# The place of the output weights' load on GpSimd's queue: ahead of the cast of x of pair 3, or behind the scaling of pair 4

## The chip, the cores and the metric

One core of one Trainium2 chip. The metric is the device time of one execution in microseconds (us); of the kernel before there are three such times, and their median is what the changed kernel is held against. Engines are named as the profile names them: PE is TensorE (matmuls), DVE is VectorE, ACT is ScalarE, POOL is GpSimd, SP is SyncE. "SPq" and "POOLq" are the instruction queues of SP and POOL where they issue transfers.

## The reference

Two layers, one behind the other. The first is a linear attention with decay over x (4 batches, 8 heads, 768 tokens, 32 values a head), with B and C of 16 states a head and a decay a for each token. It is computed in chunks: with `cum` the running sum of log a, and causal L = exp(cum_i - cum_j),

```
y_i   = sum_{j<=i} (C_i . B_j) L_ij x_j  +  exp(cum_i) C_i . state
state = decay_full * state + sum_j decay_from_j * B_j x_j
```

The second takes the 3072 tokens of y, 256 wide (heads times values), through a gated feed-forward layer of width 1536:

```
out = (relu(y @ w_gate) * (y @ w_val)) @ w_out
```

`w_out` (1536 x 256) is the matrix whose load the change moves. All inputs and the output are float32; the kernel computes in bfloat16 with float32 sums.

## The kernel before, in words

**Tiling.** Tokens go in 12 pairs of 128-token chunks (256 tokens; three pairs to a batch) through the attention, and in 6 blocks of 512 tokens (two pairs) through the feed-forward layer. For each pair: x and B, C are loaded, B and C are scaled by decays, turned so that the states lie on the partitions, `G` forms C.B (tile `g`, PE), `gevac` masks it (tile `gs`; on ACT with a causal select on POOL, line 611, and on DVE), `Dm` and `inter` form y, and `astep`/`state` adds to the carried state `A_ps`. For a block, `gv`/`gvp` make gate and val (lines 783, 786, 812), ACT takes the relu, DVE multiplies into `h`, and `fout` (line 843) forms `out` from `h` and the output weights, the tile `wo`.

**Three ways to turn B and C.** Pairs 0 to 3 are turned by PE (`turn`). Pairs 4 and 5 are turned by a transposing transfer: `scale_bc` (POOL, lines 458 and 462) writes the scaled B and C of the pair into a tile `pad`, and `dturn` (line 479, on SP's queue) turns `pad` into `TT`, which `G` of that pair reads. Pairs 6 to 11 go by `seq_scale`, `seq_turn` and `seq_part`, from the tiles `seqB` and `seqC`.

**Order.** Nothing is scheduled by a planner. The order of every engine is the order of the lines of the kernel's body, written out by hand, and `in_order` at the end pins each engine to it. So an instruction that waits holds up everything behind it on its engine; that holds for transfers as well, since a transfer is issued by an instruction of the engine named (`nc.sync.dma_start` is SP's, `nc.gpsimd.dma_start` is POOL's).

**Transfers.** SP issues nearly all loads and all stores, on one hardware queue (q1 in the profile). POOL issues the feed-forward weights, which are cast from float32 to bfloat16 on the way, on a software queue (q0): `weights` for wg and wv (line 209) in five pieces, and `weights_out(0, NF)` (line 213) for all of `wo`, 768 KB in bfloat16, in one transfer. Whoever reads any part of `wo` waits for the whole transfer.

**The stretch around the change**, lines 1020 to 1085, in the order of each engine:

- SP: `load_wide(3)`, `load_x(3)`, `load_bc(4)`, `load_bc(5)` (C and two halves of B of pairs 4 and 5, lines 117 and 121), then `load_x(4)` (line 95, two transfers), `dturn(4)`, `load_x(5)`, `load_seq(2)` (`seqB`, `seqC`, line 134), `dturn(5)`, and the loads of pair 6.
- POOL: `scale_bc(3)` (line 469), the load of `wo`, the cast of x of pair 3 (`cast_x`, line 504), the scaling of pair 4 into its `pad`, three causal selects of pair 3 (line 611), some 3 us of small set-up work for the later pairs (`seq_start`, `seq_masks`), the cast of x of pair 4, `seq_decay` (line 377), the scaling of pair 5 into its `pad`, the cast of x of pair 5.
- PE: gate and val of blocks 0 and 1 with the attention of pairs 2 and 3 between them; then the first `outs(0, 0)`, which is the first reader of `wo`; `state(4, 0)` and `G(4)`; more of `outs`; `section(4, 5)`, in which `G(5)` is; and so on to the end.

Of the kernel before, what the change touches and what calls it, by code (L numbers as in the profile page):

```python
# [29 lines left out]
def kernel(  # L30
# [21 lines left out]
    NF = DF // 128  # L52
# [35 lines left out]
    def load_x(p, hold=False, q1=nc.sync):  # L88
        b, c0 = p // PPB, 2 * (p % PPB)
        xr = raw.tile([128, 2, NH, D], FP32, tag="xr", name="xr")  # L90
        if hold:
            nc.vector.memset(xr[0:1, 0, 0, 0:1], 0.0)
        for i in range(2):
            cs = slice((c0 + i) * 128, (c0 + i + 1) * 128)
            (q1 if i else nc.sync).dma_start(  # L95
                out=xr[:, i], in_=x[b, :, cs, :].rearrange("h s d -> s h d"))
        st[p]["xr"] = xr
# [114 lines left out]
    def weights_out(f0, f1):  # L212
        nc.gpsimd.dma_start(
            out=wo[:, f0:f1, :],
            in_=moe_w_out[f0 * 128:f1 * 128, :].rearrange("(o i) m -> i o m", i=128))
# [78 lines left out]
    def diag(t, slot):  # L294

        v = t[:, slot, 0:16]
        return bass.AP(v.tensor, v.offset, [v.ap[0], (32, 4), (144, 2), (1, 16)])

    def turned(p):
        return NWIDE <= p < NRUN  # L300
# [140 lines left out]
    def scale_bc(p, eng):  # L441
        b, c0 = p // PPB, 2 * (p % PPB)
        s = st[p]
        if p >= NRUN:
            bs = att.tile([128, 2, 128], BF16, tag="bt", name="bt")
            for t in range(2):
                hs = slice(4 * t, 4 * t + 4)
                eng.tensor_tensor(
                    out=bs.rearrange("s i (q t n) -> s i t q n", q=4, t=2)[:, :, t],
                    in0=s["br"][:, :, hs],  # L450
                    in1=scaleBC[:, b, c0:c0 + 2, 0, hs].unsqueeze(3).to_broadcast(
                        [128, 2, 4, N]), op=ALU.mult)
            s["B"] = [bs[:, i] for i in range(2)]
            return
        if turned(p):
            s["pad"] = t = pads[p - NWIDE]
            for i in range(2):
                eng.tensor_tensor(
                    out=diag(t, 2 * i), in0=s["br"][:, i].rearrange("s (q t) n -> s q t n", t=2),
                    in1=scaleBC[:, b, c0 + i, 0].rearrange("s (q t) -> s q t", t=2).to_broadcast(  # L460
                        [128, 4, 2, N]), op=ALU.mult)
            eng.tensor_tensor(
                out=t[:, 4:6].rearrange("s r (h n) -> s r h n", n=N),
                in0=s["cr"].rearrange("s h r n -> s r h n"),
                in1=wD[:, p % PPB, :, 8 * b:8 * b + 8].to_broadcast([128, 2, NH, N]), op=ALU.mult)
            return
        bs = att.tile([128, 4, 128], BF16, tag="bs", name="bs")
        src = s["bcr"].rearrange("s h j r n -> s (j r) h n")
        eng.tensor_tensor(
            out=bs.rearrange("s k (h n) -> s k h n", h=NH), in0=src,  # L470
            in1=factors[p].to_broadcast([128, 4, NH, N]), op=ALU.mult)
        s["tin"] = [[bs[:, 2 * j + r] for r in range(2)] for j in range(2)]
        s["sort"] = s["tin"][0]

    def dturn(p):

        s = st[p]
        s["TT"] = att.tile([128, 6, 128], BF16, tag="TT", name="TT", bufs=2)
        nc.sync.dma_start_transpose(out=s["TT"], in_=s["pad"].rearrange("s k m -> s (k m)"))
# [21 lines left out]
    def cast_x(p, ceng):  # L501
        cast = ceng.copy if ceng is nc.scalar else ceng.tensor_copy
        xb = x_tile(p)
        cast(xb, st[p]["xr"].rearrange("s i h d -> s (i h d)"))  # L504
# [539 lines left out]
    gevac(2, 3)  # L1044
    gv_evac(*u)
    scale_bc(3, nc.gpsimd)
    weights_out(0, NF)
    cast_x(3, nc.gpsimd)
    scale_bc(4, nc.gpsimd)
    load_x(4)  # L1050
    dturn(4)
    load_x(5)
# [138 lines left out]
```

## Time and profile before

| what | value |
|---|---|
| time of the kernel before, median of 3 (lowest, highest) | 122.97 us (122.79, 123.65) |
| the profiled execution's own time | 124.32 us |
| its span, first to last instruction | 122.6 us |
| PE busy | 116.4 us, 95% of the span |
| DVE, ACT, POOL busy | 91.4, 73.9, 50.9 us |
| granted TensorE clock | full in all 40 slices of the span |
| load of `wo`, issue to landing | 768 KB, 9.7 us |

Busy time of an engine says how much it worked, and not whether anybody waited for it. The page's chain of work gives the share of the span for which each line was the last to be waited for; the timeline gives start and length of each instruction, and in brackets how long the engine had been idle before it and who ended that. Rows of the transfer queues count packets; their shares can add up to more than 100%, since packets of the two queues overlap on an engine.

### The profile page before, as it was taken

How to read it: one execution, taken by the hardware profiler on the slowest of the kernel's cores; microseconds unless marked ns; L12 is line 12 of the kernel's file. 1: busy time of each engine (PE TensorE's matmuls, PEld its weight loads, DVE VectorE, ACT ScalarE, POOL GpSimd, SP SyncE). 2: the span in 40 equal slices, each digit the busy share in tenths (PEclk: the TensorE clock that was granted, in tenths of full speed). 3: DMA queues.
4: the chain of work that ended last, by engine and by line, in shares of the span. 5: the costliest groups of instructions: out<-in, count | busy, mean ns of one | idle time of the engine just before them, and what ended most of it. 6: DMA issues, size and time to landing. Idle time of an engine off the chain costs nothing.

```text
span 122.6 us, 3330 instructions
## 1 busy us (share of the span) xinstructions
PE 116.4 (95%) x1257; PEld 78.8 (64%) x1257; DVE 91.4 (75%) x197; ACT 73.9 (60%) x147; POOL 50.9 (42%) x108
## 2 busy tenths in 40 slices
PE   7899999999999969999999999999999999999980
PEld 5576674588888758644488544588444687444870
DVE  5897999889998259699796898893897850787320
ACT  4478579888764243776745766646667735766320
POOL 7999635979355964514760820031600030000000
PEclk9999999999999999999999999999999999999999
DMA  2999997999988978979995290003100003100022
GB/s 55 200 204 203 207 201 120 139 116 186 112 150 209 216 125 133 176 148 294 158 131 118 80 125 9 5 0 134 43 3 0 0 5 128 43 0 0 2 88 86
DMA packets 63088, 13.34 MB, mean 109 GB/s; under 512 B 54688, under 2 KB 63072, under 8 KB 63072
## 3 DMA queue, kind: packets, MB, share of 16 engines
q1 hardware_dynamic: 55152, 10.33, 45.7%
q0 software_dynamic: 4272, 2.36, 14.1%
q10 hardware_dynamic: 3648, 0.44, 2.4%
q8 instruction: 10, 0.16, 0.6%
q14 instruction: 6, 0.05, 0.2%
HBM read 11.94 MB, written 3.15 MB: 123 GB/s over the span
## 4 chain that ended last, share of the span: by engine, by line
PE 68%; DMA 15%; POOL 8%; SPq 4%; ACT 1%; issue 1%; POOLq 0%; ACTq 0%
PE o L843 21%; PE gate L783 18%; PE val L786 18%; DMA TT<-pad 5%; DMA wg<-in_moe_w_gate_dram 5%; DMA xr<-in_x_dram 5%; SPq L95 3%; PE g L600 2%; PE y L745 2%; PE gate L812 2%; PE val L812 1%; POOL wg L209 1%; POOL wv L209 1%; SPq L121 1%; PE o L878 1%; PE y L735 1%
## 5 line engine op out<-in xcount | busy, mean ns | idle before, releaser
L798 DVE TENSOR_TENSOR h<-r,val 128x512 bf16<-128x512 bf16 x54 | 36.2, 684 | 11.8 <-ACT r L794 11.3
L794 ACT ACTIVATE r<-gate 128x512 bf16<-128x512 f32 x54 | 32.1, 599 | 11.8 <-PE gate L783 11.6
L783 PE MATMUL gate<-yT,wg 128*128 128x512 bf16 x108 | 32.1, 379 | 0.0
L843 PE MATMUL o<-wo,h 128*128 128x256 bf16 x276 | 32.1, 273 | 0.0
L786 PE MATMUL val<-yT,wv 128*128 128x512 bf16 x108 | 32.1, 379 | 0.0
L843 PEld LDWEIGHTS <-h 128*128 128x128 bf16 x276 | 26.3, 98 | 4.0
L611 POOL TENSOR_SCALAR_AFFINE_SELECT gs<-gs 128x512 bf16<-128x512 bf16 (+1 forms) x25 | 12.9, 542 | 32.4 <-ACT gs L628 32.3
L635 DVE TENSOR_TENSOR gs<-g,maskUT 128x512 bf16<-128x512 f32 (+1 forms) x28 | 15.3, 597 | 4.7 <-PE g L600 2.6
L786 PEld LDWEIGHTS <-wv 128*128 128x128 bf16 x108 | 10.6, 98 | 12.7
L783 PEld LDWEIGHTS <-wg 128*128 128x128 bf16 x108 | 10.4, 98 | 11.1
L628 ACT CAST gs<-g 128x512 bf16<-128x512 f32 (+1 forms) x25 | 11.1, 500 | 3.3 <-PE g L600 3.3
L825 ACT ACTIVATE r<-gate 128x512 bf16<-128x512 f32 x18 | 10.7, 604 | 2.8 <-PE gate L812 2.1
L832 DVE TENSOR_TENSOR h<-r,val 128x512 bf16<-128x512 bf16 x18 | 11.6, 678 | 0.4 <-ACT r L825 0.2
L812 PE MATMUL gate<-yT,wg 128*128 128x256 bf16 x72 | 10.8, 273 | 0.2
L812 PE MATMUL val<-yT,wv 128*128 128x256 bf16 x72 | 10.8, 273 | 0.0
L861 ACT COPY ob<-o 128x512 f32<-128x512 f32 x6 | 3.5, 586 | 9.9 <-PE o L843 9.9
L504 POOL CAST xb<-xr 128x512 bf16<-128x512 f32 x10 | 6.1, 613 | 7.7 <-DMA xr<-in_x_dram 7.6
L857 ACT COPY ob<-o 128x256 f32<-128x256 f32 x10 | 3.7, 373 | 7.8 <-PE o L843 6.8
L812 PEld LDWEIGHTS <-wg 128*128 128x128 bf16 x72 | 6.8, 98 | 1.6 <-DMA wg<-in_moe_w_gate_dram 0.4
L771 ACT CAST yT<-y 128x512 bf16<-128x512 f32 x10 | 6.2, 616 | 2.5 <-PE y L745 2.4
L812 PEld LDWEIGHTS <-wv 128*128 128x128 bf16 x72 | 7.0, 98 | 0.9
L635 DVE TENSOR_TENSOR gs<-g,maskW 128x512 bf16<-128x512 f32 (+1 forms) x6 | 3.2, 596 | 3.7 <-PE g L600 3.7
(137 smaller groups left out, 122.7 us busy)
## 6 DMA issues: line engine op xcount, KB each, us to landing
xr<-in_x_dram SPq DMA_DIRECT2D x23, 128.0 KB, 4.1
out_dram<-ob SPq DMA_DIRECT2D x6, 256.0 KB, 2.5
out_dram<-ob SPq DMA_DIRECT2D x11, 128.0 KB, 1.7
bcr<-in_C_dram SPq DMA_DIRECT2D x6, 128.0 KB, 4.1
wo<-in_moe_w_out_dram POOLq DMA_DIRECT2D x1, 768.0 KB, 9.7
seqB<-in_B_dram SPq DMA_DIRECT2D x2, 384.0 KB, 4.6
seqC<-in_C_dram SPq DMA_DIRECT2D x2, 384.0 KB, 4.9
br<-in_B_dram SPq DMA_DIRECT2D x12, 64.0 KB, 3.0
```

The costliest lines, as they stand in the source:

```text
L611: nc.gpsimd.affine_select(out=dst, in_=dst, pattern=[[0, n], [1, 2], [2, 64]] if wide else [[0, n], [1, 128]], compare_op=ALU.is_ge, fill= ...
L628: nc.scalar.copy(out=d[:, q, h], in_=g[q][:, h])
L635: nc.vector.tensor_tensor(out=d[:, q, h], in0=g[q][:, h], in1=m[:, h], op=ALU.mult)
L771: eng.copy(out=dst, in_=src)
L783: nc.tensor.matmul(out=g, lhsT=wg[:, k, fs], rhs=yT[:, k, tk], start=(k == 0), stop=(k == 1))
L786: nc.tensor.matmul(out=v, lhsT=wv[:, k, fs], rhs=yT[:, k, tk], start=(k == 0), stop=(k == 1))
L794: nc.scalar.activation(r, g, AF.Relu)
L798: nc.vector.tensor_tensor(out=fst[b][:, f], in0=r, in1=v, op=ALU.mult)
L812: nc.tensor.matmul(out=o[:, j], lhsT=w[:, k, fs], rhs=yT[:, k, tk], start=(k == 0), stop=(k == 1), skip_group_check=True)
L825: nc.scalar.activation(r, g, AF.Relu)
L832: nc.vector.tensor_tensor(out=fst[b][:, f:f + 2, u * 256:(u + 1) * 256], in0=r, in1=v, op=ALU.mult)
L843: nc.tensor.matmul(out=o[:, ts % 2], lhsT=fst[b][:, f, ts * 128:(ts + 1) * 128], rhs=wo[:, f], start=(f == 0), stop=(f == NF - 1), skip_gr ...
```

## The change

One line of the kernel's body moves down by two calls. `weights_out(0, NF)`, one instruction on POOL's queue that issues one transfer, stands behind `cast_x(3)` and `scale_bc(4)` instead of ahead of them. Size, shape and number of all instructions stay.

```diff
     scale_bc(3, nc.gpsimd)
-    weights_out(0, NF)
     cast_x(3, nc.gpsimd)
     scale_bc(4, nc.gpsimd)
+    weights_out(0, NF)
     load_x(4)
     dturn(4)
     load_x(5)
```

POOL, from the scaling of pair 3 (tile `bs`) to the causal selects of pair 3 (tile `gs`); `pad_119` is the `pad` of pair 4, `xb<-xr` the cast of x of pair 3:

```order
 L469 TENSOR_TENSOR bs<-bcr,wf_395 128x512
-L213 DMA wo<-in_moe_w_out_dram 128x12x256
 L504 COPY xb<-xr 128x512
 L458 TENSOR_TENSOR pad_119<-bcr,scaleBC 128x4x2x16 x2
 L462 TENSOR_TENSOR pad_119<-bcr,wD 128x256
+L213 DMA wo<-in_moe_w_out_dram 128x12x256
 L611 AFFINE_SELECT gs<-gs 128x512 x2
 L611 AFFINE_SELECT gs<-gs 128x256
```

The load of `wo` has moved behind four instructions of POOL, three of which read what SP's transfers of pair 4 bring in, and stands right ahead of the causal selects.

SP, from the halves of B of pair 5 to the transposing transfer of pair 5 (`pad_120`); these rows are the same before and now:

```order
L121 DMA bcr<-in_B_dram 128x8x16 x2
L95 DMA xr<-in_x_dram 128x8x32 x2
L479 DMA_TRANSPOSE TT<-pad_119 128x6x128
L95 DMA xr<-in_x_dram 128x8x32 x2
L134 DMA seqB<-in_B_dram 128x2x384
L134 DMA seqC<-in_C_dram 128x2x384
L479 DMA_TRANSPOSE TT<-pad_120 128x6x128
```

Nothing has moved on SP; the two lines L95 are the loads of x of pair 4 and of pair 5. PE, DVE and ACT have the same rows in the same order as well.

## The prediction

> **What bounds the kernel now.** I read the page first, then PE's waits, then the chain of waits over the stretch of the change, then the timelines and the queues there.
>
> ```profile
> PE 116.4 (95%) x1257; PEld 78.8 (64%) x1257; DVE 91.4 (75%) x197; ACT 73.9 (60%) x147; POOL 50.9 (42%) x108
> ```
>
> PE is the bound over the kernel as a whole, so only what makes PE wait, or stops it from waiting, can count. From 35 us to the end, PE's waits hold one row only, and its timeline shows where that is:
>
> ```profile
> PE g L600 <- DMA TT<-pad: 1.2, 1, 1.2
> ```
>
> ```profile
> 36.11 1.47 PE L843 MATMUL o<-wo,h 128*128 128x256 bf16 x12
> ...
> 43.89 0.40 PE L600 MATMUL g<-TT 32*128 32x128 bf16 x16 [1.16 <-DMA TT<-pad]
> ```
>
> So PE has one hole, 1.16 us ahead of G(5), and first touches the output weights at 36.11, without a wait. The chain from 17 to 50 us says what the hole hangs on (start, length, what):
>
> ```profile
> 25.71 3.28 SPq L95
> ...
> 29.03 6.03 DMA xr<-in_x_dram
> ...
> 35.21 0.61 POOL xb L504
> ...
> 37.46 6.38 DMA TT<-pad
> 43.84 0.05 issue
> 43.89 0.40 PE g L600 x16
> ```
>
> The second load of x of pair 4 lands at 35.06; POOL, which casts in order, stands still for it, then scales pair 5, and only then can the transposing transfer TT of pair 5 go. SP's queue and the transfer queues say why that load was slow. SP's timeline:
>
> ```profile
> 21.76 1.52 SPq L121 DMA_DIRECT2D bcr<-in_B_dram  x2
> ...
> 25.71 7.18 SPq L95 DMA_DIRECT2D xr<-in_x_dram  x2
> 32.98 1.47 SPq L479 DMA_TRANSPOSE TT<-pad  x1
> 34.50 1.20 SPq L95 DMA_DIRECT2D xr<-in_x_dram  x2
> ...
> 37.46 1.22 SPq L479 DMA_TRANSPOSE TT<-pad  x1
> ```
>
> Issuing the two loads of pair 4 held SP for 7.18 us, those of pair 5 for 1.20. The packets of the hardware queue q1 in 24 to 26 us:
>
> ```profile
> q1 hardware_dynamic: 2495, 0.22, 90.6%
> ```
>
> then both queues in 26 to 31 us:
>
> ```profile
> q0 software_dynamic: 1408, 0.72, 112.2%
> q1 hardware_dynamic: 1179, 0.08, 31.5%
> ```
>
> and in 31 to 34 us:
>
> ```profile
> q1 hardware_dynamic: 2399, 0.24, 65.5%
> q0 software_dynamic: 121, 0.06, 14.5%
> ```
>
> While q0 carries the output weights (1408 of their 1536 packets of 512 B in 26 to 31), q1 falls from some 1250 packets a us to 236. That is what starves the loads of x of pair 4.
>
> **The change part by part.** *Where the issue goes.* POOL's timeline:
>
> ```profile
> 22.76 1.07 POOL L469 TENSOR_TENSOR bs<-bcr,wf 128x512 bf16<-128x512 f32 x1
> 23.76 1.07 POOL L213 DMA_DIRECT2D wo<-in_moe_w_out_dram  x1
> 24.83 0.62 POOL L504 CAST xb<-xr 128x512 bf16<-128x512 f32 x1
> 25.41 0.77 POOL L458 TENSOR_TENSOR pad<-bcr,scaleBC 128x128 bf16<-128x128 f32 x2
> 26.14 0.61 POOL L462 TENSOR_TENSOR pad<-bcr,wD 128x256 bf16<-128x256 f32 x1
> 27.40 1.60 POOL L611 TENSOR_SCALAR_AFFINE_SELECT gs<-gs 128x512 bf16<-128x512 bf16 x3 [0.65 <-ACT gs L628]
> ...
> 35.79 0.34 POOL L377 TENSOR_TENSOR hd<-hd,pre 128x96 f32<-128x96 f32 x1
> ...
> 36.81 0.62 POOL L462 TENSOR_TENSOR pad<-bcr,wD 128x256 bf16<-128x256 f32 x1
> ```
>
> The issue's 1.07 us leaves its place, so the cast of pair 3 runs from 23.76 to 24.38. The scaling of pair 4 cannot follow at once, since it reads the two halves of B of pair 4. The issues in 22.30 to 22.47 (the first half alone) and in 22.55 to 23.2 (both halves), with the median us to landing:
>
> ```profile
> bcr<-in_B_dram SPq DMA_DIRECT2D x1, 64.0 KB, 3.3
> ```
>
> ```profile
> bcr<-in_B_dram SPq DMA_DIRECT2D x2, 64.0 KB, 3.1
> ```
>
> The first half lands at 21.76 + 3.3 = 25.06; the second, issued at about 22.5 with 2.9, at 25.4. With the 0.15 that POOL took after the landing at 35.06 to start at 35.21, the scaling starts at 25.2 and ends 1.34 later (25.41 to 26.75 before) at 26.55. The issue of the output weights starts at about 26.5 instead of 23.76: **2.7 us later**, not just the 1.95 of the instructions that it is moved past.
>
> Behind it, the three selects of pair 3 are pushed: the issue ends at 27.57, they started at 27.40. They end at 29.2 instead of 29.0. Their reader is y of pair 3 on PE:
>
> ```profile
> 29.53 0.41 PE L745 MATMUL y<-gs,xb 128*32 128x128 bf16 x16
> ```
>
> 0.3 us of cover is left, so I cost this at nothing; if the issue came 0.4 later still, each further tenth would be a tenth on PE. The set-up work behind the selects ends 0.2 later, ahead of a POOL that stood still until 35.2.
>
> *What q1 gains.* The first packets of the weights showed up at about 25.9, 2.1 us after the start of the issue; now at 28.6. In those 2.7 us q1 keeps its 1250 a us: some 3300 packets, against the 3578 that it moved from 26 to 34 before (1179 + 2399). So the rest of B of pair 5 and nearly all of x of pair 4 are through before the weights begin, and the cast of x of pair 4 no longer sets anything. What is late next is `pre`, which the step ahead of the scaling of pair 5 reads, from DVE:
>
> ```profile
> 34.39 0.21 DVE L373 STREAM_TRANSPOSE pre<-mids 128x32 f32<-128x32 f32 x1
> ```
>
> It is there at 34.60, so that step starts at 34.65; from it to the end of the scaling are 35.79 to 37.43 = 1.64 us. TT of pair 5 can go at 36.3 instead of 37.46. With the same 6.38 it lands at 42.7. PE would stand at G(5) at 43.89 - 1.16 = 42.73. Bounds: 3.0 us at least, which TT of pair 4 took:
>
> ```profile
> TT<-pad SPq DMA_TRANSPOSE x1, 3.0
> ```
>
> and at most no change, if SP is now held by the loads of x of pair 5 until 36 (rival three). I take the **full 1.16** as gained here, since the 6.38 came with a backlog of x of pair 5 on q1 that should be shorter.
>
> *What the output weights cost.* Their transfer, by the issues in 23.8 to 24.1:
>
> ```profile
> wo<-in_moe_w_out_dram POOLq DMA_DIRECT2D x1, 768.0 KB, 9.7
> ```
>
> From 23.76 it landed at 33.5, and PE came at 36.11: 2.65 us of cover, of which 2.7 are now spent. With the same 9.7 it lands at 26.5 + 9.7 = 36.2, and PE starts at 36.25, **0.15 late**. The new company on q1 (TT of pair 4 and x of pair 5) is 128-byte packets where half of it was 64-byte ones. The nearest rows for that are the gate and val weights beside loads of x, 6 to 12 us:
>
> ```profile
> q0 software_dynamic: 1594, 0.77, 95.9%
> q1 hardware_dynamic: 3245, 0.41, 48.9%
> ```
>
> 1594 packets in 6 us is 266 a us, against 1408 / 5 = 282. At that rate the 1536 packets need 5.8 us instead of 5.45, so landing at 36.55, 0.5 late with the wake-up. Bounds: nothing, if the tail after 31 us (121 packets spread over 2.4 us) is shorter, and 3 us in the second rival. I take **0.4**, nearer to the row with the same kind of company.
>
> The Trainium skill, "DMA: Bandwidth & Descriptors", section "Anatomy of one DMA", gives about 2.0 us plus the bytes at 436 GB/s for a transfer of this path: for 786,432 bytes that is 3.8 us (an estimate by that page). By that, the weights would land at 30.3, PE would not wait at all, and the sum would be the full 1.16. The row with 9.7 us disagrees by 5.9 us.
>
> *The sum.* PE's line shifts by +0.4 at 36.11; at G(5) it then arrives at 43.1, TT is there, and 1.16 are gained: 0.4 - 1.16 = -0.76. Behind 44 us PE has no wait, so the shift carries to the end. The profiled execution took 124.32 us, 1.7 around its span of 122.6; it would take 123.55. It lies 1.35 over the median of the runs shown; the same difference taken from 122.97 gives **122.2 us**. About 1%, 1.23 us, is what a measurement of this kernel tells from no change.
>
> **The rivals.**
>
> *One: the weights are in time.* If the transfer takes 9.5 us or less, PE loses nothing at 36.11 and the whole hole closes: 122.97 - 1.16 = 121.8. For it: q0 kept its rate in company of very different thickness (266 and 282). Against: 2.65 us of cover for a shift of 2.7 leave nothing over, and the page of rows shows no other hole to gain from. Half of this case lies beyond 1%.
>
> *Two, slower: PE waits for `wo` for longer than the hole.* The place is the first matmul on `wo` at 36.11, and the price decides from a landing at 37.3 (36.11 + 1.16) on. In the new place the transfer shares the engines with TT of pair 4, x of pair 5 and, if SP is through with these early, with `seqB`. In the slowest us beside other loads, 6 to 7 us, q0 had
>
> ```profile
> q0 software_dynamic: 183, 0.09, 67.0%
> ```
>
> packets. Halfway between 183 and the 282 above is 232: 6.6 us of packets, landing at 37.4, no change. At 183 throughout it is 8.4 us, landing at 39.1, a wait of 3.0 and 122.97 + 1.9 = 124.9. I price this rival at 200 a us: 7.7 us, landing at 38.4, a wait of 2.4: 124.2. Against it: the 6-us mean is 266, and the tail of the transfer may be the same whatever goes beside it.
>
> *Three: the hole stays.* The weights now run from 28.6 to 34 and then their tail to 36.2. x of pair 5 is issued about then and may hold SP until 36, as x of pair 4 did until 32.9. `seqB`, `seqC` and TT of pair 5 would go when they went before, and TT would land where it landed: 122.9, no change. For it: 7.18 us of hold under q0 in the rows. Against: TT of pair 4 and both loads would have to be starved all through.
>
> **How the numbers follow.** The forecast 0.40 (its own range 121.9 to 122.7), rival one 0.22, rival two 0.24, rival three 0.14. Faster by over 1% (below 121.74): most of half of rival one, and the forecast's lower edge, 0.10 + 0.07 = 0.17. Slower by over 1% (above 124.20): rival two counts in its price and beyond, and what I have not seen behind 44 us, 0.20. Within 1%: 0.63. The range holds the forecast, rivals one and three, and rival two up to its price: 121.6 to 124.2.
>
> **What would show it.** Right: the issue L213 starts at 26.4 to 26.7 on POOL; SP issues x of pair 4 in under 3 us instead of 7.18; the scaling of pair 5 starts at 34.6 to 35.2 and not at 36.1; PE's waits lose the row for TT, or most of it, and gain one of 0.1 to 1 us for `wo` at 36.1. The two waits then sum to less than 1.16. Wrong: a wait for `wo` of 1.2 us and more (rival two), no wait for `wo` at all (rival one), a second line of SP held until 36 and TT landing at 43.5 or later (rival three), or a new wait of PE behind 44 us, where I have counted none.

## The result, and the profile after

The changed kernel takes 124.76 us (median of 5) against 122.98 for the kernel before: a ratio of 1.0125, with a 95% interval of 1.0094 to 1.0157. The forecast was 122.2 us in a range of 121.6 to 124.2. The change is slower, because PE now waits for `wo`, as rival two had it. That the time comes near rival two's worst price (124.9) is partly luck: that price was a wait of 3.0 us less a gain of 1.16, and the runs below show a shorter wait, with no such gain to stand against it.

Some executions, of the kernel before as well, take some 2 to 3% longer, which the ratios leave out and the medians of the experiments do not, and the profile of the changed kernel (127.70 us) is of one of these, so it is read by intervals and not by its span. Its first gate matmuls come at 12.37 instead of 9.90, and so they do in a later profile of the kernel before (e17, the second row):

```profile
12.37 0.98 PE L812 MATMUL gate<-yT,wg 128*128 128x256 bf16 x4
```

```profile
12.36 1.03 PE L812 MATMUL gate<-yT,wg 128*128 128x256 bf16 x4
```

PE's waits in the changed kernel from 15 us on:

```profile
PE o L843 <- DMA wo<-in_moe_w_out_dram: 0.9, 1, 0.9
PE val L786 <- ACT ob L857: 0.8, 1, 0.8
```

The row for TT is gone, as forecast. In its place are a wait for `wo` and a second, 16 us later, for ACT, which had waited 2.78 us for a store to free an output tile. The load of `wo` in that profile (issue at 28.06) and the transposing transfer of pair 4, from the issues in 29.1 to 30.5:

```profile
wo<-in_moe_w_out_dram POOLq DMA_DIRECT2D x1, 768.0 KB, 11.7
TT<-pad SPq DMA_TRANSPOSE x1, 11.0
```

They took 9.7 and 3.0 before. SP's timeline there:

```profile
27.26 1.70 SPq L95 DMA_DIRECT2D xr<-in_x_dram  x2
29.06 1.52 SPq L479 DMA_TRANSPOSE TT<-pad  x1
30.63 4.41 SPq L95 DMA_DIRECT2D xr<-in_x_dram  x2
35.08 4.44 SPq L134 DMA_DIRECT2D seqB<-in_B_dram  x1
39.56 0.47 SPq L134 DMA_DIRECT2D seqC<-in_C_dram  x1
40.13 1.22 SPq L479 DMA_TRANSPOSE TT<-pad  x1
```

x of pair 4 is issued in 1.70 us, against 7.18. But SP, free sooner, now puts the transposing transfer of pair 4 on its queue just ahead of the packets of `wo`, and then stands for 8.85 us on the next two lines. The transposing transfer of pair 5, the last row, comes behind them.

### The profile page after: what moved, and what is told of

It reads as the page before. It is cut to its first block, busy times and chain, and to the rows that moved or that the text cites. A ratio compares the mean times of both kernels' runs of the same rounds, so it can differ in the third digit from the quotient of the medians.

```text
span 126.0 us, 3330 instructions
## 1 busy us (share of the span) xinstructions
PE 119.8 (95%) x1257; PEld 81.1 (64%) x1257; DVE 91.2 (72%) x197; ACT 73.8 (59%) x147; POOL 50.9 (40%) x108
## 4 chain that ended last, share of the span: by engine, by line
PE 79%; DMA 13%; DVE 2%; POOL 1%; ACT 1%; issue 1%; ACTq 0%; POOLq 0%
PE o L843 23%; PE val L786 17%; PE gate L783 17%; DMA wo<-in_moe_w_out_dram 9%; DMA out_dram<-ob 4%; PE w L194 3%; PE g L600 3%; PE gate L812 3%; PE y L745 3%; PE val L812 2%; DVE h L798 1%; PE o L878 1%; PE y L735 1%; PE decs L236 1%; DVE gs L635 1%
## 5 line engine op out<-in xcount | busy, mean ns | idle before, releaser
L798 DVE TENSOR_TENSOR h<-r,val 128x512 bf16<-128x512 bf16 x54 | 35.8, 683 | 13.2 <-ACT r L794 12.6
L843 PEld LDWEIGHTS <-h 128*128 128x128 bf16 x276 | 26.1, 98 | 5.2 <-DMA wo<-in_moe_w_out_dram 1.2
L786 PEld LDWEIGHTS <-wv 128*128 128x128 bf16 x108 | 10.5, 98 | 13.7 <-issue 1.1
L783 PEld LDWEIGHTS <-wg 128*128 128x128 bf16 x108 | 10.3, 98 | 11.1
L825 ACT ACTIVATE r<-gate 128x512 bf16<-128x512 f32 x18 | 10.7, 604 | 2.8 <-PE gate L812 2.4
L832 DVE TENSOR_TENSOR h<-r,val 128x512 bf16<-128x512 bf16 x18 | 11.5, 677 | 0.3 <-ACT r L825 0.2
L812 PE MATMUL gate<-yT,wg 128*128 128x256 bf16 x72 | 11.2, 280 | 0.1
L448 POOL TENSOR_TENSOR bt<-br,scaleBC 128x128 bf16<-128x128 f32 x12 | 4.6, 403 | 4.5 <-DMA br<-in_B_dram 4.5
## 6 DMA issues: line engine op xcount, KB each, us to landing
wo<-in_moe_w_out_dram POOLq DMA_DIRECT2D x1, 768.0 KB, 11.7
```

The costliest lines, as they stand in the source:

```text
L783: nc.tensor.matmul(out=g, lhsT=wg[:, k, fs], rhs=yT[:, k, tk], start=(k == 0), stop=(k == 1))
L786: nc.tensor.matmul(out=v, lhsT=wv[:, k, fs], rhs=yT[:, k, tk], start=(k == 0), stop=(k == 1))
L798: nc.vector.tensor_tensor(out=fst[b][:, f], in0=r, in1=v, op=ALU.mult)
L812: nc.tensor.matmul(out=o[:, j], lhsT=w[:, k, fs], rhs=yT[:, k, tk], start=(k == 0), stop=(k == 1), skip_group_check=True)
L825: nc.scalar.activation(r, g, AF.Relu)
L832: nc.vector.tensor_tensor(out=fst[b][:, f:f + 2, u * 256:(u + 1) * 256], in0=r, in1=v, op=ALU.mult)
```

## The experiments

Theory T: the transposing transfer of pair 4 and the load of `wo` slow each other when they run together. Rival Q: any company of SP's queue would do. Rival L: `wo` is late, and not slower.

**e1, the changed kernel again.** No edit.

> The changed kernel itself, for a second profile, since in the first one the first 14 us ran 2.6 us later than in the kernel before, ahead of the place of the change. Theory T (the transposing transfer of pair 4 now runs beside the load of wo, and each slows the other): wo from issue to landing 11 to 12.5 us, the transposing transfer of pair 4 over 8 us, a wait of PE for wo of 0.8 to 2.5 us. Rival Q (the load of wo is slowed by any traffic of SP's queue, and the transposing one is nothing special) expects the same here. Rival L (it is only late, not slowed; the 11.7 of the first profile came with the late start): wo back at 9.5 to 10.2 us, a wait under 0.6 us. Time 124.5 to 125.0 by all.

Ratio 1.0148 (1.0083 to 1.0214). `wo` 11.9 us, the transposing transfer 10.4, and on PE

```profile
39.14 2.74 PE L843 MATMUL o<-wo,h 128*128 128x256 bf16 x12 [2.53 <-DMA wo<-in_moe_w_out_dram]
```

L falls: the load takes 2.2 us longer than the 9.7 of before, besides starting 3.4 later (27.19 against 23.76). A further cost is in the row itself: 12 matmuls take 2.74 us, against 1.47 in the kernel before. The stretches around it (the figure right behind the times and counts of the five engines is the granted clock, PEclk):

```profile
36.60:39.10 2.50, 0.01 (x1) 0.00 (x0) 0.89 (x2) 0.20 (x1) 0.16 (x1) 0.93 1.10 141
39.10:42.00 2.90, 2.86 (x14) 1.94 (x14) 0.00 (x0) 0.00 (x0) 0.61 (x1) 0.50 1.08 319
```

The granted clock is 0.50 behind the wait of 2.53 us, for 2.9 us, which costs PE another 1.3. Behind waits of 0.94, 1.23 and 1.54 us in other profiles (the changed kernel, e11, e15) it stayed full. The Trainium skill, "TensorE: Matmul & The Clock Gate", section "Part 1: The HAM clock gate", has the clock fall after at least one idle window of some 3.4 us; this row disagrees. A mean of 0.93 over 2.50 us is 0.35 us at half, so the clock fell some 2.1 us into the wait.

**e2, a plain copy in place of the transposing transfer of pair 4.**

```diff
+        if p == 4:
+            nc.sync.dma_start(out=s["TT"], in_=s["pad"])
+            return
         nc.sync.dma_start_transpose(out=s["TT"], ...)
```

> The changed kernel with the transposing transfer of pair 4 replaced by a plain copy of the same tile between the same places (so the C.B products of pair 4 are formed from an unturned tile). T: wo lands 9.5 to 10.3 us after its issue, x of pair 5 in under 6 us instead of 9.9, PE waits for wo at most 0.6 us, the time falls to 122.0 to 123.2. Q: wo still takes over 11 us and the time stays at 124.3 to 125.0.

123.16 us, 0.9951 of the kernel before (0.9900 to 1.0002). The load of `wo`, issued at 26.13:

```profile
wo<-in_moe_w_out_dram POOLq DMA_DIRECT2D x1, 768.0 KB, 9.8
```

and no wait of PE at 36.13. The queues in 30 to 35 us, first of e2, then of e1, whose load had begun 1.06 us later:

```profile
q0 software_dynamic: 1328, 0.67, 105.0%
q1 hardware_dynamic: 1090, 0.32, 36.1%
```

```profile
q0 software_dynamic: 1032, 0.53, 92.8%
q1 hardware_dynamic: 718, 0.18, 44.4%
```

In the same 5 us e1 moves 1032 packets of the weights to e2's 1328, and fewer of SP's queue as well: together they lose, and neither gives way to the other. Two single us of e1, 33 to 34 and 36 to 37, say how:

```profile
q0 software_dynamic: 239, 0.12, 88.1%
q1 hardware_dynamic: 239, 0.06, 46.3%
```

```profile
q0 software_dynamic: 16, 0.01, 26.9%
q1 hardware_dynamic: 14, 0.00, 11.2%
```

In the first the two queues move equal numbers, 239 and 239, as if the engines took one packet of each in turn (the Trainium skill, "DMA: Bandwidth & Descriptors", section "Queues, rings and completion order", has an engine go round robin between the queues that have work; this row agrees). In the second almost nothing moves on either queue. Q falls for this kernel: the same tile moved without turning leaves the load at 9.8. The plain copy is itself held up, though (8.4 us, and x of pair 5 took 8.3, where T said under 6), and its packets are of some 1.4 KB (144 in 0.20 MB in e5), where those of e1 in 33 to 34 us have some 250 bytes (239 in 0.06 MB). So e2 alone does not part the turning from the size of the packets.

**e3, block 0 multiplied with the gate weights instead of `wo`**, so that PE needs `wo` some 14 us later.

```diff
-                rhs=wo[:, f], start=(f == 0), stop=(f == NF - 1),
+                rhs=wo[:, f] if b else wg[:, f // 6, f % 6 * DM:(f % 6 + 1) * DM],
+                start=(f == 0), stop=(f == NF - 1),
```

> The changed kernel, but the output matmuls of token block 0 take the gate weights (a tile of the same size that landed long before) in place of wo, so that PE's first need of wo comes some 14 us later. The transfers stay as they are. If the wait for wo is the loss: 0.9 to 2.5 us faster than the changed kernel, 122.2 to 123.8, and what is then left over the kernel before (less 1.16 for the closed hole) is the price of the late stores. If the late stores (the wait of ACT for the store of an output tile, 2.78 us in the profile, which cost PE 0.8) carry it: no faster than 124.3, since PE then runs into that wait earlier.

124.64 us, 1.0090 (1.0032 to 1.0148), above the 122.2 to 123.8 that was expected if the wait for `wo` is the loss. By the ratios some four tenths of e1's loss went, but the two intervals overlap. `wo` took 12.4 us with nobody waiting for it, so PE's wait is not what slows it. PE's waits from 35 us on:

```profile
PE g L600 <- DMA TT<-pad: 2.6, 2, 1.5
```

The transposing transfer of pair 4, 11.3 us, is late for its own reader by 1.12 us, and that of pair 5, behind it, by 1.51. In the changed kernel the wait for `wo` covers both. PE waits for no late store here.

**e4, the kernel before with the transposing transfer of pair 4 issued ahead of x of pair 4.**

```diff
-    load_x(4)
     dturn(4)
+    load_x(4)
     load_x(5)
```

> The kernel before with one exchange on SP's queue: the transposing transfer of pair 4 is issued ahead of the loads of x of pair 4 instead of behind them, so it runs beside the load of wo, which stands at its old place. T: wo takes 11 us and more instead of 9.7 although it starts where it did, the transposing transfer over 6 us instead of 3.0, x of pair 4 lands later than 36, and the hole of PE ahead of the C.B products of pair 5 grows: 124 to 127. Q: the load of wo has as much company as before, 9.3 to 10.2 us, and the time moves by less than 1 us.

124.69 us, 1.0055 (0.9990 to 1.0120), unclear. T's number for `wo` was wrong and Q's held: 9.5 us, not 11. There is no hole ahead of G(5); PE's only wait behind 15 us is one of 1.17 for ACT. Issued at 26.99, behind B of pair 5 and when the packets of `wo` had been running since 26, the transposing transfer was held up like anything else on q1 (8.7 us) and met only the end of the load. So it is not enough that both are under way. That the transposing transfer has to be at the head of its queue when the load begins, as it is in the changed kernel, is what e7 puts to the test. And a standstill comes up here too, with no packet of `wo` left. The load had landed at 33.5, the transposing transfer landed at 35.7 and x was waiting, and in 34 to 35 us all that moved was

```profile
q1 hardware_dynamic: 37, 0.01, 7.0%
```

**e5, the pair by itself.** A kernel of eight stages of loads, one after the other.

> A kernel of its own that computes nothing of the reference: eight stages, each begun when the one before has landed. Loads: wo alone; the transposing transfer of a pad alone; wo with the transposing transfer; wo with a plain copy of the pad; wo with the two loads of x of a pair; wo with the transposing transfer and x; wo alone; wo with the transposing transfer. Theory T (the transposing transfer and the load of wo slow each other): wo alone 7.5 to 9 us, the transposing transfer alone 3 to 4 us; together wo over 9.5 us and the transposing transfer over 6 us; with the plain copy or x, wo within 1 us of wo alone. Rival Q (any company of SP's queue): wo with x is as slow as or slower than wo with the transposing transfer.

`wo` alone 7.8 and 7.6 us; the transposing transfer alone 2.8; both together `wo` 9.4 and 8.2 and the transposing transfer 5.2 and 4.9, with the plain copy `wo` 7.5, with x 8.5, with both x and the transposing transfer 8.5. T's numbers (over 9.5 and over 6) missed, and the stages do not decide: issued at once on an idle SP, the transposing transfer had sent 766 of its 800 packets before those of `wo` began.

**e6, half a step: `wo` between the cast of pair 3 and the scaling of pair 4.**

```diff
-    weights_out(0, NF)
     cast_x(3, nc.gpsimd)
+    weights_out(0, NF)
     scale_bc(4, nc.gpsimd)
```

> The load of wo between the cast of x of pair 3 and the scaling of pair 4, half a step of the change: its issue starts at 24.4 instead of 23.8 or 26.5. SP reaches x of pair 4 before the weights' packets begin, the transposing transfer of pair 4 still waits for the scaling, which now ends 0.5 us later than in the changed kernel. T: SP is held by x of pair 4 as before, so the transposing transfer meets only the end of the load; wo lands 9.3 to 10.2 us after its issue, at 34.6 or so, no wait for it; the hole ahead of the C.B products of pair 5 stays within 0.5 us of 1.16; time within 0.6 us of the kernel before. A theory by which each tenth of lateness of wo costs the same would put it at a fifth of the way, +0.3 us.

123.33 us, 1.0011 (0.9977 to 1.0044): no change. `wo` 10.5 us (T: 9.3 to 10.2), the transposing transfer 6.3, no wait for `wo`, a hole of 0.73. The issue came at 24.14, only 0.4 later than before, and the +0.3 us of a loss that grows with lateness lies within the interval. So this run does not part the two.

**e7, the changed kernel with the transposing transfer of pair 4 behind x of pair 5.**

```diff
-    dturn(4)
     load_x(5)
+    dturn(4)
     load_seq(2, nc.sync)
```

> The changed kernel with one exchange on SP's queue: the transposing transfer of pair 4 behind the loads of x of pair 5 instead of ahead of them. T: while the load of wo runs, SP's queue carries x of pair 5 alone, which does it no harm; wo lands 9.4 to 10.4 us after its issue, PE waits for it at most 0.5 us, the transposing transfer of pair 4 lands at 36 to 38 in 3 to 4 us, and the hole ahead of pair 5 is under 0.6 us: 122.0 to 123.3 us. Q: wo still takes over 11 us, 124.3 or more.

123.81 us, 0.9989 (0.9944 to 1.0034). One exchange on SP takes the whole loss back, with `wo` issued as late as in e2 (26.15), and 2.4 us later than in the kernel before:

```profile
wo<-in_moe_w_out_dram POOLq DMA_DIRECT2D x1, 768.0 KB, 9.7
```

So lateness of this size is not enough for the loss. T's time for the transposing transfer was wrong: issued at 28.89, it took 8.5 us and not 3 to 4, and it was under way during most of the load. Its packets stood behind those of x of pair 5 (in 30 to 31 us q1 moved none at all), so the load was nearly through when they came. It is the order that decides, not only that both are under way. The profiled execution has neither wait to speak of (0.21 us), and ran in 122.94 us, close to the median of the kernel before (122.98). The hole is closed here, and yet the kernel is no faster; that question is taken up in e16.

**e8, `wo` at its old place, x of pair 4 ahead of B and C of pair 5 on SP's queue.**

```diff
     load_bc(4)
+    load_x(4)
     load_bc(5)
```

> The kernel before, wo at its old place, with the loads of x of pair 4 issued ahead of B and C of pair 5 on SP's queue. If the hole of 1.16 hangs on x of pair 4 being starved by wo, as the prediction had it: x of pair 4 lands by 30, the hole shrinks to under 0.5 us, wo stays at 9.3 to 10.2 us, time 121.8 to 122.8. If the next starved load takes its place (B of pair 5, wanted at 35): the hole stays at 0.8 to 1.5 us, the time within 0.4 of the kernel before.

123.02 us, 0.9963 (0.9932 to 0.9994). `wo` took 8.8 us and PE had no wait from 35 us on. By itself that is a gain of 0.4%; e12, which only adds output tiles to it, does not repeat it.

**e9, the pair by itself, with x ahead of it,** so that the transposing transfer meets the packets of `wo`.

> A kernel of its own that computes nothing of the reference, as the one before it, in which the transposing transfer was through before the packets of wo began. Now two loads of x stand ahead of it on SP's queue and two behind, so that its packets meet those of wo as in the changed kernel. Stages: wo with x alone; wo with x, transposing transfer, x; the same with a plain copy; x, transposing transfer, x without wo; then the second, third and first again. T: wo 8.3 to 9.2 us with x alone and with the plain copy, 10 us or more with the transposing transfer in both of its stages; the transposing transfer 3 to 5 us without wo and over 7 with it. Q: wo the same within 0.7 us in all stages.

`wo` with x 9.8 and 8.5; with x and the transposing transfer 10.4 and 10.4; with x and the plain copy 10.3 and 9.4. The transposing transfer took 9.2 and 9.1 with `wo`, 3.3 without it. T and Q each get part: the transposing transfer takes nearly three times as long, but the load itself is slowed by 0.1 to 1.0 us more than by a plain copy. The standstills of the kernel did not come up.

**e10, `wo` later still, behind the causal selects of pair 3.**

```diff
     gvp_evac(*u)
+    weights_out(0, NF)
     seq_start()
```

> The load of wo later still, behind the causal selects of pair 3 (issue at about 29 instead of 26.5). If lateness were all, wo lands 2.5 us later than in the changed kernel, PE waits some 4 us for it and the time is 126 or more. By T the transposing transfer of pair 4 is through, or nearly, before the packets of wo begin (31): it takes 3 to 5 us, wo 9 to 10.3 us, landing at 38.3 to 39.3, the same as in the changed kernel although it starts 2.5 us later; PE waits 2 to 3.2 us, time 124.3 to 126.5.

129.64 us, 1.0480 (1.0415 to 1.0546). The transposing transfer of pair 4, now through before the weights, took 3.2 us as T said. `wo` took 10.7, above T's 9 to 10.3, beside `seqB` and, at its end, the transposing transfer of pair 5 (issue at 36.52, 5.0 us); what made it so long these runs do not part. It landed at 39.8, 0.7 us later than in e1, although it was issued 1.9 later. PE waited 3.39 us, more than T's 2 to 3.2, and was then granted about half its clock for 5.9 us:

```profile
39.80:45.70 5.90, 5.87 (x43) 4.08 (x44) 2.41 (x5) 0.86 (x2) 1.25 (x3) 0.52 0.62 84
```

At 0.52 these 5.9 us hold some 2.8 us of lost clock (an estimate: 5.9 x 0.48). The forecast of 124.3 to 126.5 left this fall out.

**e11, the changed kernel with six output tiles instead of three.**

> The changed kernel with six instead of three buffers for the output tile, so that ACT does not wait for a store. T (wo and the transposing transfer carry the loss): within 0.4 us of the changed kernel, 124.2 to 125.0. If the late stores, which cost PE 0.8 in one profile of the changed kernel, carry part in most executions: 0.6 to 1.0 us faster than the changed kernel.

125.79 us, 1.0113 (1.0067 to 1.0158), the changed kernel's loss within its interval. The late store is no part of it that can be measured. `wo` 11.2, the transposing transfer 10.6, PE's wait 1.23.

**e12, e8 with six output tiles.**

> The kernel with x of pair 4 ahead of B and C of pair 5 (wo at its old place), and six buffers for the output tile: the best version that the runs point to. The first part gave 0.996 of the kernel before; the buffers should add nothing where PE does not wait for a store: 122.2 to 122.9, ratio 0.992 to 0.998.

123.88 us, 1.0013 (0.9971 to 1.0054); `wo` 8.8, no wait. No faster than the kernel before, so e8's 0.4% is not a gain that these runs establish.

**e13 and e14, 10 and 24 matmuls on constants in the place of PE's wait.**

```diff
     gvp(1, 1, 10)
+    keep_warm(10)      # e14: 24
     outs(0, 0)
```

> The changed kernel with 10 matmuls on constants (1.1 us of PE at full clock) put between the last gate and val matmuls and the first use of wo. In the profiles PE waited there 0.9, 1.2 and 2.5 us. If PE's wait in the timed executions is 1.1 us or more, the filling costs nothing, and where the wait is long enough to bring the granted clock down it may save up to 1.3 us of half clock: within 0.4 of the changed kernel run beside it, or faster. If the wait in the timed executions is mostly short (0.3) and the loss lies elsewhere, 0.8 slower.

> The same with 24 matmuls (2.6 us at full clock). If the wait is 2.5 us in most timed executions, no slower than the changed kernel, and faster by up to 1.3 where the clock came down. If it is 1.2 in most, slower by 1.4 (2.6 - 1.2), 125.9 to 126.4.

Ratios 1.0272 (1.0196 to 1.0347) and 1.0197 (1.0160 to 1.0233). Both are slower than expected of a filling that costs nothing, and their intervals overlap, so 10 matmuls and 24 are not told apart. In the profile of e13 PE still waited 1.22 us behind the filling, in that of e14 not at all. How long PE waits in the timed executions can't be told from them.

**e15, the changed kernel a third time, beside these two.**

> The changed kernel once more, beside these two, as what they are held against, and for one more profile of the load of wo in company of the transposing transfer: 11.0 to 12.5 us from issue to landing by T, a wait of PE of 0.9 to 2.6 us; 124.3 to 125.0 us.

`wo` 11.9, the transposing transfer 10.3, a wait of 1.54. There is no ratio for this run.

**e16 to e18, the kernel before, three more profiles.** The profile that the prediction was made from is of an execution of 124.32 us, and e7 with hardly a hole ran in 122.94.

> The kernel before itself, for another profile. The profile on which the prediction rests is of an execution of 124.32 us, 1.35 over the median, and the two kernels in which PE has neither the hole ahead of the C.B products of pair 5 nor a wait for wo ran in 122.64 and 122.87 when profiled. Theory H (the hole of 1.16 is a trait of that one execution; in the usual one it is shorter or absent): an execution of 122.6 to 123.4 us with a hole of 0 to 0.5. Rival: the hole is there in every execution, 0.9 to 1.4, also in one of about 123.

> The same once more: by H the time and the hole move together, 122.6 plus the hole, within 0.4; by the rival the hole stays at 0.9 to 1.4 whatever the time.

> The same a third time: by H 122.6 plus the hole, within 0.4; by the rival a hole of 0.9 to 1.4 whatever the time.

None of the three has a hole. In e16, an execution of 122.58 us, PE's only wait is at its very start, and it goes through the first use of `wo` and G(5) without one:

```profile
35.93 1.47 PE L843 MATMUL o<-wo,h 128*128 128x256 bf16 x12
...
42.49 0.40 PE L600 MATMUL g<-TT 32*128 32x128 bf16 x16
```

SP and POOL in e16:

```profile
24.98 4.62 SPq L95 DMA_DIRECT2D xr<-in_x_dram  x2
29.70 3.20 SPq L479 DMA_TRANSPOSE TT<-pad  x1
...
36.39 1.22 SPq L479 DMA_TRANSPOSE TT<-pad  x1
```

```profile
33.68 0.61 POOL L504 CAST xb<-xr 128x512 bf16<-128x512 f32 x1 [1.92 <-DMA xr<-in_x_dram]
34.72 0.34 POOL L377 TENSOR_TENSOR hd<-hd,pre 128x96 f32<-128x96 f32 x1 [0.44 <-DVE pre L373]
35.02 0.76 POOL L458 TENSOR_TENSOR pad<-bcr,scaleBC 128x128 bf16<-128x128 f32 x2
```

x of pair 4 is starved here too, 4.62 us of hold, but lands before `pre` does: the step ahead of the scaling of pair 5 waits for DVE, not for x. The transposing transfer of pair 5 itself differs more: it went 1.07 us earlier than in the first profile (36.39 against 37.46) and took 3.8 us against 6.38. In the other two, of 126.24 and 126.26 us, the whole excess over e16 is there before the first use of `wo` (39.72 and 39.74 against 35.93), and there is no hole; so H's sum of 122.6 plus the hole misses for them, while its point, no hole, holds in all three. `wo` took 8.8, 8.5 and 9.2 us, against 9.7 in the first profile.

## Why the prediction was wrong, point by point

**"So PE has one hole, 1.16 us": the first step that failed.** The row was right and was of one execution, 1.35 us over the median. The prediction saw that difference, put it down to nothing, and took the gain from the median, in which the hole has already gone. Three further profiles of the kernel before have none. The profiled executions of e7 and e8, with a hole of 0.21 and none, took 122.94 and 122.64 us, and the ratios of these kernels, 0.9989 and 0.9963, have intervals that leave out the 0.9906 that closing a hole of 1.16 in most executions would give. The term of -1.16 should have been near 0.

**"TT of pair 5 can go at 36.3 instead of 37.46": the second step that failed.** In e1 POOL was done with the scaling of pair 5 at 36.76, but SP had stood on the load of `seqB` for 5.76 us, and the transposing transfer went at 38.63, later than before. That is the mechanism of rival three, in another line of SP. That it landed at 43.0, near the forecast 42.7, is luck: it took 4.4 us and not the 6.38 of the sum. In e3 it went at 39.27, took 6.1 us, and PE waited 1.51 for it.

**"From 23.76 it landed at 33.5 ... I take 0.4": the term that was mis-sized.** The start was nearly right: 26.1 to 27.2 in e1, e2, e3, e7, e11 and e13, forecast 26.5. The transit was not. In the three profiles of the changed kernel and in those of e11, e13 and e14, which issue the same transfers, `wo` took 11.7, 11.9, 11.9, 11.2, 11.6 and 11.7 us, and in e3 12.4, where the forecast took 9.95. PE's lateness, with what the filling of e13 and e14 covered counted in, was 0.94, 2.53, 1.54, 1.23, 2.5 and 1.0 us in the first six, 1.6 on average. The median of 122.98 plus 1.6 is 124.6, an estimate; measured are 124.76. It is not more than that: the three profiles of the changed kernel are of executions of 127 us and more, so how long PE waits in one of 124.7 is not shown.

**The price of company.** The forecast named the transposing transfer as part of the new company, counted it as 128-byte packets like x, and took gate and val weights beside loads of x as the nearest row. In e1 the packets of q1 in 33 to 34 us have some 250 bytes, and that company was what decided. Rival two had the wait and, at its worst, 183 packets a us and a landing at 39.1. That e1 landed at 39.1 is luck in part: its load was issued 0.7 us later than forecast, and it lost time in a near standstill and not at an even rate. The rival was given 0.24, with a price of 124.2 from inside its bounds.

**What held.** x of pair 4 goes out in under 3 us (1.70, 1.24); the scaling of pair 5 waits for `pre` and starts at 35.43 in e1, 0.2 behind the forecast's 34.6 to 35.2; no profile of the changed kernel has a wait for TT; the selects of pair 3 cost nothing; `wo` is what PE meets instead.

**What was not priced.** Behind the waits of 2.53 us (e1) and 3.39 us (e10) the granted clock was about half, which cost another 1.3 and some 2.8 us. And a freed SP does not only load sooner: the next thing in its order comes sooner as well, here the worst company for the load that had just been moved.

**What stays open.** Why the queues come to a standstill in the kernel. e4 has one when no packet of `wo` is left, so it does not need the load; that `wo` is late because a standstill falls into its transfer fits e1, e4 and e7, but no run here makes or removes a standstill alone. By themselves (e9) the transposing transfer took about as long beside the load (9.2 us), but `wo` at most 1 us more than beside a plain copy. e2 and e7 show that in this kernel the loss comes from the transposing transfer of pair 4 being at the head of SP's queue when the load of `wo` begins; they do not show what happens in the engines.

## What to carry to other kernels

Before a hole in one profile is spent as a gain, hold the profiled execution's own time against the median: an execution 1.35 us over the median with one hole of 1.16 may be showing what the others lack. When a transfer is moved back, ask what its neighbours on the other queue will now be doing when it runs; the queue that it had held up gets further ahead, and a different transfer comes beside it. In this kernel a transposing transfer at the head of its queue was poor company for a large load that somebody waited for.

## What the runs showed of the hardware that was not expected

- A transposing transfer of 192 KB took 2.8 us alone (e5) and 3.3 between loads of x (e9), and 9.9 to 11.3 when it began just ahead of the load of `wo`. The load took 8.5 to 9.7 us in the kernel before, and 11.2 to 12.4 then.
- In one us of e1 (36 to 37) the two queues together moved 30 packets, where either alone has some 340 (q0, e7 in 30 to 31 us) or 1250 (q1, before in 24 to 26). In one us of e4 q1 moved 37, with q0 empty.
- 12 matmuls took 2.74 us instead of 1.47 after 2.53 us without work for PE; after 1.54 they took 1.49.
- In five profiles (the changed kernel, e14, e15, e17, e18) PE's first 4 gate matmuls of 128x256, at 12.4 us, took 0.98 to 1.03 us, against 0.61 in the profile of before, while the granted clock is 1.00 in 12 to 13.5 us.
